# A decode layer on one core: feed-forward weights loaded last, gate and up in column form, another layout for w_down

## The chip, the cores and the metric

The kernel runs on one core of one Trainium2 chip. The metric is the device time of one execution in microseconds (us). A core has a tensor engine (PE, with its weight loads shown as PEld), a vector engine (DVE), a scalar engine (ACT), a general engine (POOL) and a sync engine (SP) that here issues the loads. Loads run on 16 DMA engines. "Span" is the time from the first to the last instruction in the profile; it is about 1.8 us shorter than the time. All runs quoted are in the fast state, and every kernel below gave a correct result.

## The reference, cut to what matters

One token, width 512. Attention over a cache of 65,536 positions with 32 query heads on 8 key/value heads of 128, then a gated feed-forward layer of 1,792 hidden units.

```python
x = A_x
h = x + attention(layernorm(x), k_cache, v_cache, wq, wo)   # K and V: 8 x 65536 x 128 bf16 each, 134 MB each
g = layernorm(h) @ w_gate        # 512 x 1792
u = layernorm(h) @ w_up          # 512 x 1792
out = h + (sigmoid(g) * u) @ w_down                          # 1792 x 512
```

Nearly all the bytes are K and V, each read once. The feed-forward weights are 3 x 1.83 = 5.5 MB of 282 MB.

## The kernel before

All loads go through one queue. K, V and w_q take turns in a ring of four slots of 4 MB; a load waits until the slot's last user is done. `Prog` writes operations down and derives the semaphore waits from the names in `deps`.

```python
order = [("wq", 0)]
order += [("K", b) for b in range(NR)]                 # NR = 4 blocks per head, NB = 32 blocks
for b in range(NR, NB):
    order += [("K", b), ("V", b - NR)]
order += [("V", NB - 4), ("wgu", 0), ("V", NB - 3), ("V", NB - 2), ("V", NB - 1)]
...
if k == "wq":
    ... # w_q into the ring, and directly behind it the whole of w_down into its own buffer:
    B_w_down[0:1536, :].rearrange("(c p r) n -> p c (r n)", p=128, r=4)   # wd0: 3 x 4 rows per partition
    B_w_down[1536:1792, :].rearrange("(p r) n -> p (r n)", r=2)           # wd1: 2 rows per partition
...
if ld == ("V", NB - 4):
    ... # w_o, in pieces of 1 KB, into the buffer that the scores no longer need
```

After the last V block: rest of PV, head output (`po`, `ox`, `o2`), projection with w_o, layer norm (`hc` is the centred row as a column), and the feed-forward layer in row form. There `hc` is the stationary operand of one column and the weights stream past, so the result is a row:

```python
for i, bank in enumerate((GB, UB)):                    # gate, up
    for kt in range(4):
        for c in range(4):                             # 512 columns each, on 4 strips of 32 PE columns
            matmul(ps(bank, 0, n, 32*c, 32*c+1), lhsT=hc[:, kt:kt+1], rhs=wv[:, kt, c*512:c*512+n], ...)
sg = tanh(rstd * gate)             # 128x512 on ACT       (the sigmoid by way of tanh)
up = rstd * up                     # 128x512 on DVE
hh = (sg + 1) * up                 # 128x512 on DVE
# 14 tiny matmuls turn the rows of hh into columns, 4 copies take them to hhT
for kt in range(14):
    for g in range(4):
        matmul(ps(YB, 0, 128, 32*g, 32*g+1), lhsT=hhT[:, kt:kt+1], rhs=wd_v[:, kt, g*128:(g+1)*128], ...)
# copy to y_sb, output DMA
```

## Time and profile before

| | before |
|---|---|
| time, median of 3 (then of 4) runs | 681.42 us (680.79) |
| span of the profiled run | 678.4 us |
| last V completion in the trace | 665.27 us |
| span behind it | 13.1 us |

Lines of the page of the kernel before: the span, the DMA share in 40 slices (9 is 90% or more), the rate in each slice, and the totals.

```profile
span 678.4 us, 5646 instructions
...
PE 391.9 (58%) x2506; PEld 158.8 (23%) x2506; DVE 353.6 (52%) x405; ACT 34.3 (5%) x92; POOL 5.7 (1%) x10
...
DMA  8999999999999999999999999999999999999990
GB/s 346 441 433 430 433 432 433 430 433 432 433 430 429 433 425 433 428 433 430 431 432 431 431 432 431 432 433 428 433 432 431 433 432 427 430 423 359 433 416 24
DMA packets 15640, 282.68 MB, mean 417 GB/s; under 512 B 1153, under 2 KB 5249, under 8 KB 6785
```

PE and DVE are busy little more than half of the time, and the stream of loads moves at about 432 GB/s from the second slice on. A kernel like this takes the time of the stream, plus what stands before the first byte, plus what stands behind the last. The last slice shows 24 GB/s: there nothing is loaded.

The windows view of the end of the stream. After the stretch and its length come busy time and count of PE, PEld, DVE, ACT and POOL, then the granted PE clock, the mean share of the 16 DMA engines and the rate.

```profile
659.00:660.00 1.00, 0.17 (x4) 0.00 (x0) 0.00 (x0) 0.00 (x0) 0.00 (x0) 0.65 0.97 410
...
661.00:662.00 1.00, 0.00 (x0) 0.00 (x0) 0.00 (x0) 0.00 (x0) 0.00 (x0) 1.00 0.54 229
...
663.00:664.00 1.00, 1.00 (x16) 0.36 (x16) 0.00 (x0) 0.00 (x0) 0.00 (x0) 0.56 0.12 49
...
665.00:666.00 1.00, 1.00 (x16) 0.15 (x8) 0.00 (x0) 0.00 (x0) 0.00 (x0) 0.50 0.00 0
```

The stream doesn't end at once. A load is split over 16 engines, and it has landed when the last of them is done. The 16 completions of the last V piece come in groups: seven at 661.1 to 661.6, seven at 663.0 to 663.5, two at 665.06 and 665.27.

The timeline of what follows (start, length, engine, line, operation, output and inputs, count):

```profile
662.87 3.50 PE L401 MATMUL PS<-ring,PT_sb 128*16 128x512 bf16 x32 [3.70 <-DMA ring<-in_A_v_cache_dram]
...
669.28 0.16 DVE L453 SCALAR_TENSOR_TENSOR hc<-PS,hT 128x4 bf16<-128x4 f32 x1 [0.48 <-PE PS L259]
...
669.50 2.76 PE L462 MATMUL PS<-ring,hc 128*1 128x512 bf16 x29 [0.25 <-DVE hc L453]
...
672.74 0.75 DVE L472 TENSOR_SCALAR up<-PS,rstd 128x512 f32<-128x512 f32 x1 [2.65 <-remote]
673.52 0.69 DVE L473 SCALAR_TENSOR_TENSOR hh<-sg,up 128x512 bf16<-128x512 f32 x1
...
674.27 0.32 PE L478 MATMUL PS<-ones_c,hh 1*128 1x1 bf16 x14 [1.16 <-DVE hh L473]
...
675.01 0.95 PE L491 MATMUL PS<-wd_sb,hhT 128*1 128x128 bf16 x56 [0.43 <-ACT hhT L487]
676.02 0.29 DVE L495 CAST y_sb<-PS 128x128 bf16<-128x128 f32 x1 [1.11 <-PE PS L491]
676.33 0.62 SPq L496 DMA_DIRECT2D out_dram<-y_sb  x1
```

Every step waits for the one before it, from V's landing to the output. All weights were in memory long before, so in these 13.1 us the DMA engines stand idle, but for the output.

### The profile page before, as it was taken

How to read it: one execution, taken by the hardware profiler on the slowest of the kernel's cores; microseconds unless marked ns; L12 is line 12 of the kernel's file. 1: busy time of each engine (PE TensorE's matmuls, PEld its weight loads, DVE VectorE, ACT ScalarE, POOL GpSimd, SP SyncE). 2: the span in 40 equal slices, each digit the busy share in tenths (PEclk: the TensorE clock that was granted, in tenths of full speed). 3: DMA queues.
4: the chain of work that ended last, by engine and by line, in shares of the span. 5: the costliest groups of instructions: out<-in, count | busy, mean ns of one | idle time of the engine just before them, and what ended most of it. 6: DMA issues, size and time to landing. Idle time of an engine off the chain costs nothing.

```text
span 678.4 us, 5646 instructions
## 1 busy us (share of the span) xinstructions
PE 391.9 (58%) x2506; PEld 158.8 (23%) x2506; DVE 353.6 (52%) x405; ACT 34.3 (5%) x92; POOL 5.7 (1%) x10
## 2 busy tenths in 40 slices
PE   2587596555566655455665655466665644662145
PEld 2432232122222222122222222122221212221112
DVE  3289875564447655463556744465555644470001
ACT  0200100020002000020000200020000200020000
POOL 3000000000000000000000000000000000000000
PEclk9889797777888767688887778887766778885567
DMA  8999999999999999999999999999999999999990
GB/s 346 441 433 430 433 432 433 430 433 432 433 430 429 433 425 433 428 433 430 431 432 431 431 432 431 432 433 428 433 432 431 433 432 427 430 423 359 433 416 24
DMA packets 15640, 282.68 MB, mean 417 GB/s; under 512 B 1153, under 2 KB 5249, under 8 KB 6785
## 3 DMA queue, kind: packets, MB, share of 16 engines
q1 hardware_dynamic: 15616, 282.34, 97.6%
q8 instruction: 19, 0.31, 0.2%
q14 instruction: 5, 0.03, 0.0%
HBM read 282.33 MB, written 0.00 MB: 416 GB/s over the span
## 4 chain that ended last, share of the span: by engine, by line
issue 98%; DVE 1%; PE 0%; another core or an unknown queue 0%; POOL 0%; POOLq 0%; ACT 0%; ACTq 0%; DVEq 0%
DVE rows_i L244 0%; PE PS L491 0%; DVE up L472 0%; DVE hh L473 0%; PE PS L259 0%; POOLq L112 0%; POOL rstd L270 0%; PE PS L478 0%; DVE lsel L247 0%; DVE y_sb L495 0%; DVE sel_f L248 0%; DVE zrow L239 0%; POOL iota_i L232 0%; DVE ident L236 0%
## 5 line engine op out<-in xcount | busy, mean ns | idle before, releaser
L338 PE MATMUL PS<-ktw 128*128 128x512 bf16 x1024 | 294.4, 449 | 205.7 <-DVE ktw L324 203.3
L324 DVE STREAM_TRANSPOSE ktw<-ring 128x1024 f32<-128x1024 f32 x256 | 292.0, 1208 | 192.7 <-DMA ring<-in_A_k_cache_dram 192.7
L338 PEld LDWEIGHTS PS<-ktw 128*128 128x128 bf16 x1024 | 107.0, 110 | 389.6 <-DVE ktw L324 249.9
L401 PE MATMUL PS<-ring,PT_sb 128*16 128x512 bf16 x1024 | 69.9, 420 | 28.0 <-DMA ring<-in_A_v_cache_dram 28.0
L325 DVE TENSOR_REDUCE M_sb<-PS 128x1 f32<-128x512 f32 x32 | 22.1, 692 | 47.5 <-PE PS L338 47.5
L401 PEld LDWEIGHTS PS<-ring,PT_sb 128*16 128x16 bf16 x1024 | 28.2, 113 | 60.1 <-DMA ring<-in_A_v_cache_dram 32.4
L415 DVE CAST O<-PS 128x4 bf16<-128x4 f32 x8 | 1.3, 163 | 57.5 <-PE PS L412 57.5
L358 ACT ACTIVATE negmax<-PS 128x1 f32<-128x1 f32 x8 | 1.4, 171 | 554.9 <-PE PS L356 554.9
L370 DVE STREAM_TRANSPOSE PT_sb<-P_sb 128x512 bf16<-128x512 bf16 x32 | 21.8, 712 | 11.9 <-ACT P_sb L367 11.9
L367 ACT ACTIVATE P_sb<-PS,negmax 128x512 bf16<-128x512 f32 x32 | 21.6, 686 | 0.3
L289 PE MATMUL PS<-ring,xz 128*32 128x128 bf16 x128 | 9.3, 248 | 6.4 <-DMA ring<-in_A_wq_dram 6.4
L289 PEld LDWEIGHTS PS<-ring,xz 128*32 128x32 bf16 x128 | 9.2, 113 | 6.5 <-issue 6.5
L425 PE MATMUL PS<-O,ktw 128*128 128x1 bf16 x128 | 3.7, 165 | 9.6 <-DMA ktw<-in_A_wo_dram 9.4
L412 PE MATMUL PS<-sel_bf,po_sb 128*128 128x4 bf16 x32 | 2.0, 167 | 12.4 <-ACT po_sb L409 12.4
L409 ACT ACTIVATE po_sb<-PS,rl 128x512 bf16<-128x512 f32 x8 | 5.6, 695 | 56.4 <-PE PS L401 56.4
L349 PE MATMUL PS<-identf,gm 128*1 128x128 f32 x16 | 3.0, 271 | 7.8 <-DVE gm L347 7.8
L270 POOL TENSOR_TENSOR rstd<-ve,nhalf 128x1 f32<-128x1 f32 x2 | 1.1, 553 | 664.4 <-DVE ve L268 664.4
L367 ACT ACTIVATION_READ_ACCUMULATOR P_sb<-PS,negmax 128x1 f32 x32 | 6.5, 203 | 0.0
L356 PE MATMUL PS<-one_f,gmrep 1*128 1x1 f32 x16 | 3.0, 256 | 5.0 <-DVE gmrep L353 5.0
L425 PEld LDWEIGHTS PS<-O,ktw 128*128 128x128 bf16 x128 | 3.5, 103 | 9.8 <-DMA ktw<-in_A_wo_dram 9.4
L412 PEld LDWEIGHTS PS<-sel_bf,po_sb 128*128 128x128 bf16 x32 | 1.3, 96 | 17.1 <-ACT po_sb L409 17.1
L351 DVE TENSOR_REDUCE gmj<-PS 1x4 f32<-1x128 f32 x8 | 2.2, 278 | 3.8 <-PE PS L349 3.8
(67 smaller groups left out, 50.3 us busy)
## 6 DMA issues: line engine op xcount, KB each, us to landing
ring<-in_A_k_cache_dram SPq DMA_DIRECT2D x32, 4096.0 KB, 29.7
ring<-in_A_v_cache_dram SPq DMA_DIRECT2D x31, 4096.0 KB, 35.4
ring<-in_A_wq_dram SPq DMA_DIRECT2D x1, 4096.0 KB, 12.4
ktw<-in_A_wo_dram SPq DMA_DIRECT2D x1, 4096.0 KB, 22.3
ring<-in_A_v_cache_dram SPq DMA_DIRECT2D x1, 3072.0 KB, 38.2
ring<-in_B_w_gate_dram SPq DMA_DIRECT2D x1, 1792.0 KB, 26.4
ring<-in_B_w_up_dram SPq DMA_DIRECT2D x1, 1792.0 KB, 14.8
wd_sb<-in_B_w_down_dram SPq DMA_DIRECT2D x1, 1536.0 KB, 15.8
```

What stands on the lines that cost most here:

```text
L289: op("pe", lambda e, kt=kt, n=n, last=last: e.matmul(ps(1, 0, 128, 0, 32), lhsT=xz[:, kt * 63 + 31 - n: kt * 63 + 63 - n], rhs=wq_v[:, kt, ...
L324: op("dve", lambda e, d=dst, sr=src: e.transpose(d, sr), deps, f"T{b}.{c}")
L325: op("dve", lambda e: e.tensor_reduce(M_sb[:, b % 8:b % 8 + 1], ps(b % NS, 0, 512), AX.X, ALU.max), [f"S{b}"], f"mx{b}")
L338: op("pe", lambda e, n=n, je=je, c=c: e.matmul(ps(b % NS, 0, 512), lhsT=w_ap(h, je, c), rhs=kt_ap(n, je), start=(c == 0 and je == 0), stop ...
L349: op("pe", lambda e: e.matmul(ps(MISC, 0, 128, 0, 1), lhsT=gm[:, k:k + 1], rhs=identf[:, :], start=True, stop=True), [f"gm{h}", "identf", ...
L356: op("pe", lambda e: e.matmul(ps(MISC, 128, 129), lhsT=gmrep[0:1, :], rhs=one_f[0:1, 0:1], start=True, stop=True), [f"gmrep{h}", "onef"], ...
L367: op("act", lambda e, b=b: e.activation(P_sb[:, (b % 4) * 512:(b % 4 + 1) * 512], ps(b % NS, 0, 512), AF.Exp, bias=negmax[:, k:k + 1], sca ...
L370: op("dve", lambda e, b=b: e.transpose(PT_sb[:, (b % 8) * 512:(b % 8 + 1) * 512], P_sb[:, (b % 4) * 512:(b % 4 + 1) * 512]), [f"E{b}", f"P ...
L401: op("pe", lambda e, lhsT=lhsT, tq=tq, t0=t0, c=c: e.matmul(ps(bank, 0, 512, 32 * tq, 32 * tq + 16), lhsT=lhsT, rhs=ring[:, s * SLOT + t0 ...
L409: op("act", lambda e: e.activation(po_sb[:, :], ps(PO_BANKS[k], 0, 512), AF.Copy, scale=rl[:, k:k + 1]), [f"PV{NR * h + NR - 1}", f"rl{h}" ...
L412: op("pe", lambda e, t=t: e.matmul(ps(MISC, 140, 144), lhsT=po_sb[:, t * 128:(t + 1) * 128], rhs=sel_bf[:, 4 * t:4 * t + 4], start=(t == 0 ...
L425: op("pe", lambda e, j=j, nt=nt, last=last: e.matmul(ps(YT, nt, nt + 1), lhsT=wo_v[:, j, nt * 128:(nt + 1) * 128], rhs=O2[:, j:j + 1], sta ...
```

## The change

The intent: let the feed-forward weights be the last loads, so that they stream in while the serial part after V runs; and give the feed-forward layer a form whose result is a column at once, so that neither turns nor wide activations stand behind the last load. The diff, cut to its core:

```diff
-        order += [("V", NB - 4), ("wgu", 0), ("V", NB - 3), ("V", NB - 2), ("V", NB - 1)]
+        order += [("V", NB - 4), ("V", NB - 3), ("V", NB - 2), ("V", NB - 1), ("wg", 0), ("wu", 0), ("wd", 0)]
...
-        dma("sp", lambda e: e.dma_start(x4[:, :], ...), "x", name="x")
+        dma("act", lambda e: e.dma_start(x4[:, :], ...), "x", name="x")
...   (w_down's two loads behind w_q are gone; each of gate and up gets its own slot and semaphore)
+            elif k == "wd":
+                src = B_w_down.rearrange("(p r) n -> p r n", p=128)          # 14 rows per partition
+                for i, (r0, r1) in enumerate([(0, 12), (12, 14)]):
+                    d2, sr = dst[:, r0*D:r1*D].rearrange("p (r n) -> p r n", n=D), src[:, r0:r1, :]
+                    if i == 1:
+                        d2, sr = dst[:, r0*D:r1*D], src.rearrange("(o p) r n -> o p (r n)", o=8)[:, :, r0*D:r1*D]
+                    dma("sp", lambda e, d2=d2, sr=sr: e.dma_start(d2, sr), f"wd{i}", ...)
...   (row form, turns and copies are gone)
+        for i, (nm, bank) in enumerate((("wg", GB), ("wu", UB))):
+            for r in range(14):
+                for kt in range(4):
+                    lhsT = bass.AP(tensor=ring, offset=s0 + kt*FF + r, ap=[[NSLOT*SLOT, 128], [14, 128]])
+                    matmul(ps(bank, r, r + 1), lhsT=lhsT, rhs=hc[:, kt:kt+1], start=(kt == 0), stop=(kt == 3))
+        sg  = tanh(rstd * gate)            # 128x14 on ACT
+        sg2 = (sg + 1) * rstd              # 128x14 on DVE
+        hhT = up * sg2                     # 128x14 on DVE, already in columns
```

Partition p holds the hidden units 14p to 14p+13. So the weights of one matmul are every 14th column of w_gate: steps of 14 elements, 28 bytes.

## The prediction

> **What bounds the kernel now.** The stream of loads. The page gives 282.68 MB at a mean 417 GB/s; nearly every slice from the second on shows about 432 GB/s, while PE is busy 58% and DVE 52%. The DMA queue's waits show SP waiting for DVE to free K slots (446 us in sum), but without a gap in the stream, so they cost nothing. Three places are slower: the first 3 us, the stretch of w_o (351 GB/s at 610 to 620 us), and the end. The windows view shows the DMA share falling to 0.71 at 660 us and 0.12 at 663: of the 16 completions of the last V piece, seven come at 661.1 to 661.6, seven at 663.0 to 663.5, two stragglers at 665.06 and 665.27. Then comes a serial tail, in the timeline: PV's rest to 666.4, head output, projection and layer norm (hc at 669.4), gate and up to 672.7, up and hh to 674.2, 14 turns and copies to 675.0, down to 676.0, copy, output DMA to 678.4. So 13.1 us of the 678.4 us span have no load under them.
>
> **What the change does.** No byte is removed; 5.5 MB of weights move behind V. At 432 GB/s this is 12.7 us, so V31 lands at about 652.1, and PV, head output, projection and norm (4.1 us to hc) run under the loading of the gate. Landings: hc ready 656.2, gate 656.3, up 660.6, 12 rows of w_down 664.2, the last 2 about 665.3. Attention starts about 4.2 us earlier without w_down before K0; that alone gains nothing.
>
> Gate and up become 2x56 matmuls with 128x128 weights. The projection has the same form at 28 ns each (112 in 3.06 us, windows view), so 1.6 us each: up done at 662.2. The activations shrink from 128x512 (0.69 to 0.75 us) to 128x14 (small DVE operations take 0.16 us); turns and copies vanish. hhT is ready near 662.7, before w_down. After the last landing remain 8 matmuls (0.3 us), copy 0.3, output 2.4: 3.1 instead of 13.1.
>
> x on ACT's queue lets w_q be issued at 0.74 instead of 1.18 us: 0.4 us.
>
> The last 2 rows are split by 8. The Trainium skill, "DMA: Bandwidth & Descriptors", section on why a DMA increments its semaphore by 16, says that the DMA then uses the lowest 8 engines. The two groups of completions fit that: the early ones get these 262 KB, about 1.2 us. If a straggler is among them, it ends 0.6 us later than with 16.
>
> **On the critical path.** 10 us of tail, plus 0.4, minus up to 0.6. Predicted span 668.5; time 671.4 us (1.5% less), range 669.4 to 674.0. Faster by over 2%: 0.04; within 2%: 0.95; slower: 0.01.
>
> **Right or wrong.** V31 lands near 652; gate starts near 656.3, up on its DMA; the final matmuls wait for w_down's DMA, not DVE; the stream has no gap; 3.1 us follow the last landing.
>
> **What would make it wrong.** The new weights are read with 28-byte steps. "SBUF — State Buffer", section on the DMA port swizzle, names 16-byte lines, each crossing of which costs; no trace here shows such a step for weights (8 bytes in the turns cost nothing: 14 in 0.23 us). At 60 ns each it is still hidden; at 110 ns the time would be 675.8. Also: stragglers lagging more in the new order, or w_down's issue, which waits for PV30, coming late (expected 651, needed about 660).

## The result

| | before | changed |
|---|---|---|
| time, median of 4 runs | 680.79 us (680.13 to 681.5) | 670.07 us (669.99 to 670.13) |
| ratio | | 0.9842, 95% interval 0.9825 to 0.9859 |
| span | 678.4 | 668.3 |
| last completion of a load | 665.27 | 664.72 |
| span behind it | 13.1 | 3.6 |

All outputs are right. The ratio is the mean time of one kernel's runs over that of the other's of the same rounds, so it isn't quite the ratio of the medians quoted. The change is clear of noise, and inside the 2% band that counts as "same". The medians differ by 10.7 us and the spans by 10.1, because the profiled run of the kernel before was one of its quicker ones (680.17 us); its runs spread over 1.4 us here, those of the changed kernel over 0.14. Times are compared by medians below, and spans only tell where the time goes.

The page of the changed kernel:

```profile
span 668.3 us, 5771 instructions
...
DMA  9999999999999999999999999999999999999996
GB/s 377 436 429 421 437 432 431 423 437 432 431 429 431 433 431 426 432 437 430 426 430 435 436 421 435 432 431 427 431 431 434 428 432 433 429 433 362 430 414 247
DMA packets 15384, 282.70 MB, mean 423 GB/s; under 512 B 1152, under 2 KB 5248, under 8 KB 6400
```

The bytes and the rate in the middle are the same. The last slice moved from 24 to 247 GB/s: the stream now reaches far into what was the idle end. Its timeline:

```profile
648.96 3.34 PE L400 MATMUL PS<-ring,PT_sb 128*16 128x512 bf16 x32 [3.73 <-DMA ring<-in_A_v_cache_dram]
...
655.23 0.16 DVE L451 SCALAR_TENSOR_TENSOR hc<-PS,hT 128x4 bf16<-128x4 f32 x1 [0.48 <-PE PS L258]
...
656.06 3.50 PE L460 MATMUL PS<-hc,ring 128*128 128x1 bf16 x56 [0.87 <-DVE ve L267]
...
660.47 3.52 PE L460 MATMUL PS<-hc,ring 128*128 128x1 bf16 x56 [0.38 <-DMA ring<-in_B_w_up_dram]
664.03 0.17 DVE L471 TENSOR_TENSOR hhT<-PS,sg 128x14 bf16<-128x14 f32 x1 [3.89 <-PE PS L460]
...
664.26 1.67 PE L476 MATMUL PS<-ring,hhT 128*1 128x128 bf16 x56 [0.26 <-DVE hhT L471]
665.97 0.29 DVE L480 CAST y_sb<-PS 128x128 bf16<-128x128 f32 x1 [1.77 <-PE PS L476]
666.29 0.66 SPq L481 DMA_DIRECT2D out_dram<-y_sb  x1
```

From the completions in the trace, V landed at 651.41, gate at 655.92, up at 660.42, the first 12 rows of w_down at 664.09 and the last two at 664.72. The gate matmuls carry the label of a layer-norm step (`ve`), but nothing of that feeds them; they start 0.14 us after gate's completion, so gate's DMA released them. The part from PV to `hc`, which cost 4 us in the open, now lies under the gate's load.

Two things in these lines aren't as predicted. The 56 matmuls of gate, and of up, take 3.5 us, not 1.6. And the down matmuls were released by DVE (hhT), 0.17 us after w_down had landed, not by the DMA. They also take 1.67 us, where before they took 0.95. The windows view of just these 56, before:

```profile
675.00:676.10 1.10, 0.95 (x56) 0.78 (x56) 0.08 (x1) 0.00 (x0) 0.00 (x0) 1.00 0.00 0
```

and in the changed kernel:

```profile
664.20:666.00 1.80, 1.67 (x56) 1.38 (x56) 0.03 (x2) 0.00 (x0) 0.00 (x0) 0.50 0.05 9
```

The granted PE clock was 1.00 in the first case and 0.50 in the second. The new layout of w_down isn't what costs: form_step8 below has the old layout and the old buffer, and down takes 1.66 us there, also at 0.50.

### The profile page after: what moved, and what is told of

Read it like the earlier page. It is cut to its first block, busy times and chain, and to the rows that moved or that the text cites. A ratio compares the mean times of both kernels' runs of the same rounds, so it can differ in the third digit from the quotient of the medians.

```text
span 668.3 us, 5771 instructions
## 1 busy us (share of the span) xinstructions
PE 397.0 (59%) x2572; PEld 165.3 (25%) x2572; DVE 352.2 (53%) x402; ACT 33.7 (5%) x90; POOL 5.7 (1%) x10
## 4 chain that ended last, share of the span: by engine, by line
DMA 69%; DVE 25%; PE 5%; issue 0%; ACT 0%; SPq 0%
DMA ring<-in_A_k_cache_dram 61%; DVE ktw L323 24%; DMA ring<-in_A_v_cache_dram 5%; DMA ring<-in_B_w_up_dram 4%; PE PS L337 3%; PE PS L460 1%; DVE M_sb L324 1%; PE PS L400 1%; DVE PT_sb L369 0%; PE PS L476 0%; ACT P_sb L366 0%; SPq L203 0%; PE PS L348 0%; PE PS L355 0%; SPq L228 0%
## 5 line engine op out<-in xcount | busy, mean ns | idle before, releaser
L460 PE MATMUL PS<-hc,ring 128*128 128x1 bf16 x112 | 7.0, 198 | 1.2 <-DVE ve L267 0.9
L460 PEld LDWEIGHTS PS<-hc,ring 128*128 128x128 bf16 x112 | 6.9, 159 | 1.8 <-DVE ve L267 0.9
```

Source lines behind the costliest of these rows:

```text
L460: op("pe", lambda e, lhsT=lhsT, kt=kt, r=r, bank=bank: e.matmul(ps(bank, r, r + 1), lhsT=lhsT, rhs=hc[:, kt:kt + 1], start=(kt == 0), stop ...
```

## The experiments

The theory: time = end of the stream + what stands behind its last landing. The order of the loads gives nearly all of the gain by hiding the serial part, and the column form matters only through the little that it leaves behind the last landing. The rival: the column form is faster in itself and the order merely allows it.

### Order alone

The old arithmetic; only the loads moved (w_down in its old layout, x still on SP).

```diff
+        order += [("V", NB - 4), ("V", NB - 3), ("V", NB - 2), ("V", NB - 1), ("wg", 0), ("wu", 0), ("wd", 0)]
-                       ["hc", "wgu0", "wgu1"] if kt == 0 and c == 0
+                       ["hc", "wg" if i == 0 else "wu"] if kt == 0 and c == 0
```

> The kernel before with only the loads moved: gate, up and w_down last, arithmetic in the old row form, x still on SP. Theory (the gain is that the serial part after V runs under the loads): V's last piece near 652, w_down's last near 665.2; gate matmuls from 656, up from 660.5; about 5 us of old form after it, span near 669.5 to 671, so 7.5 to 9 of the 10.1 us. Rival (the column form is what shortens the tail, the order only allows it): under 4 us of gain, span over 674.

Measured: 671.16 us (before 681.32 on the same chip), ratio 0.9852, span 669.2. That is 10.2 us; the changed form measured below (after_step8) came to 670.31. The timeline of its end:

```profile
656.28 1.87 PE L460 MATMUL PS<-ring,hc 128*1 128x512 bf16 x16 [0.38 <-DVE mo L263]
...
660.68 1.45 PE L460 MATMUL PS<-ring,hc 128*1 128x512 bf16 x13 [2.52 <-DMA ring<-in_B_w_up_dram]
...
665.13 1.66 PE L489 MATMUL PS<-ring,hhT 128*1 128x128 bf16 x56 [0.66 <-DMA ring<-in_B_w_down_dram]
...
667.16 0.62 SPq L494 DMA_DIRECT2D out_dram<-y_sb  x1
```

All that the old row form does after up's landing (660.63), with turns and wide activations, is over at 664.8, before w_down's last landing (664.99). The final matmuls wait for the DMA of w_down. So order alone brings over nine tenths of the change, and the rival falls. It gained slightly more than I had expected (span 669.5 to 671).

What the column form adds in the new order can be read from x_sp below, which has the same order and also issues x on SP: 670.38 us, so 0.8 us less than order_only. Even this is an upper bound, since order_only also starts its down matmuls only when both pieces of w_down are there, while the changed kernel starts at the first.

### Form alone

The old order of loads, with w_down still before K0, but as 14 rows per partition; gate and up in column form.

```diff
+                    lhsT = bass.AP(tensor=ring, offset=s0 + kt*FF + r, ap=[[NSLOT*SLOT, 128], [14, 128]])
+                    matmul(ps(bank, r, r + 1), lhsT=lhsT, rhs=hc[:, kt:kt+1], ...)      # loads as before
```

> The kernel before with only the arithmetic changed: loads in the old order, gate and up in column form with 28-byte steps, w_down as 14 rows per partition loaded before K0. Theory: exposed, the 112 weight loads cost 63 ns each, 7.0 us against 3.2 for the old gate and up, of which the dropped turns and shorter activations give back about 2.3 us, and down runs at the lower granted clock: span 679.5 to 681, slower than before by 1 to 2.5 us. Rival (the column form is faster in itself): span 677 or less.

Measured: 683.14 us against 681.32, ratio 1.0028 (1.0013 to 1.0043), span 681.4: slower by 1.8 us. That is the loss expected, with a span 0.4 us above the range given. Gate and up in its timeline:

```profile
669.54 3.52 PE L459 MATMUL PS<-hc,ring 128*128 128x1 bf16 x56 [0.26 <-DVE mo L263]
...
673.53 3.52 PE L459 MATMUL PS<-hc,ring 128*128 128x1 bf16 x56
```

In the open, the new form is slower than the old one: 7.0 us for gate and up, where the old form ran from 669.5 to 672.7.

### What the 63 ns per matmul are

3.52 us / 56 = 63 ns. The projection in the same column form with contiguous weights took 28 ns each, at the same granted clock of 0.50 (timeline of the kernel before):

```profile
626.93 3.15 PE L425 MATMUL PS<-O,ktw 128*128 128x1 bf16 x112 [9.37 <-DMA ktw<-in_A_wo_dram]
```

The Trainium skill, "SBUF — State Buffer", section "Door 1: The DMA port swizzle", says that SBUF is read in lines of 16 bytes and that each access that crosses to a new line pays. Steps of 28 bytes cross at every element. To test this, the hidden units were mapped as in the kernel before (four units per partition in three groups, then two), which gives steps of 8 and 4 bytes, and w_down's old loads.

```diff
-                    lhsT = bass.AP(tensor=ring, offset=s0 + kt*FF + r, ap=[[NSLOT*SLOT, 128], [14, 128]])
+                    q, stp = (r // 4 * 512 + r % 4, 4) if r < 12 else (1536 + r - 12, 2)
+                    lhsT = bass.AP(tensor=ring, offset=s0 + kt*FF + q, ap=[[NSLOT*SLOT, 128], [stp, 128]])
```

In the old order:

> As form_only, but hidden units mapped to partitions as before (4 and 2 rows of w_down per partition), so the weights are read in steps of 8 and 4 bytes instead of 28. If the step costs: weight loads near 28 to 32 ns each, gate and up 3.2 to 3.6 us together, span 3.4 us below form_only (676 to 677.5). If the 63 ns come from the column form or the clock and not from the step: the same as form_only within 0.5 us.

Measured: 680.29 us, span 678.6, 2.8 us below form_only. Gate and up:

```profile
669.82 1.98 PE L461 MATMUL PS<-hc,ring 128*128 128x1 bf16 x56 [0.26 <-DVE hc L452]
...
672.27 1.97 PE L461 MATMUL PS<-hc,ring 128*128 128x1 bf16 x56
```

That is 35 ns each instead of 63, at the same granted clock (0.50 in the windows of both). The starts of the matmuls in the traces show it more sharply, free of what the first and the last one add: they follow each other every 60 ns with steps of 28 bytes (changed kernel), every 33 ns with steps of 8 bytes, and every 27 ns with steps of 4 bytes, which are the last 8 of each 56 in form_step8; the projection with contiguous weights also has 27. So the step costs, as the skill says; the numbers are from here. That the line is 16 bytes long is not shown: no step between 8 and 28 was run. Against the kernel before, this form comes out about even: the ratio is 0.9985 (0.9969 to 1.0002). Dropping the turns is worth nothing clear while it stands in the open: by the timelines, from up's end to the start of down takes 0.3 us instead of 2.3, but gate and up take 4.4 us instead of 3.2, and down, at the lower clock, 1.66 instead of 0.95. The fall was somewhat smaller than the 3.4 us expected, because 35 ns isn't 28, and because V happened to land 0.3 us later (665.22 against 664.94).

The same mapping in the new order:

> The changed kernel with steps of 8 and 4 bytes instead of 28, and w_down loaded in pieces of 4 KB and 2 KB as before. If the step costs: up done near 662.2 instead of 664.0, hhT near 662.4; then the down matmuls wait for the DMA of w_down (664.1), not for DVE, and the span falls by only 0.1 to 0.3 us (668.0 to 668.2), because w_down's landing is the next limit. If the step doesn't cost: up still done at 664.0, span 668.3.

Measured: 670.31 us, span 668.3, as the changed kernel.

```profile
660.22 1.98 PE L459 MATMUL PS<-hc,ring 128*128 128x1 bf16 x56 [1.90 <-DMA ring<-in_B_w_up_dram]
...
664.03 1.85 PE L475 MATMUL PS<-ring,hhT 128*1 128x128 bf16 x56 [1.84 <-DMA ring<-in_B_w_down_dram]
```

Up is done 1.8 us earlier, and nothing is gained: the down matmuls now wait 1.84 us for w_down. In the changed kernel up's end and w_down's landing nearly coincide, so taking one away leaves the other. The span didn't fall by the 0.1 to 0.3 us expected.

### Smaller pieces of w_down

```diff
-    WD_SPLIT = [(0, 12), (12, 14)]
+    WD_SPLIT = [(0, 4), (4, 8), (8, 12), (12, 14)]        # on top of after_step8; one wait for each piece
```

> As after_step8, with the first 12 rows of w_down in three loads of 4 rows, each with its own wait. Theory (what is left is the wait of 56 matmuls for one landing of 12 rows, 1.85 us of PE after 664.0): 32 to 48 of the 56 matmuls run before the last landing (664.5), down ends near 664.9 instead of 665.9, span 667.2 to 667.5, 0.8 to 1.1 us below after_step8. Rival (the loads lose time by being smaller, or PE at the lower clock is the limit anyway): 668.2 or more.

Measured: 669.25 us, span 667.4.

```profile
660.26 1.97 PE L459 MATMUL PS<-hc,ring 128*128 128x1 bf16 x56 [1.93 <-DMA ring<-in_B_w_up_dram]
...
662.50 1.02 PE L475 MATMUL PS<-ring,hhT 128*1 128x128 bf16 x32 [0.26 <-DVE hhT L470]
...
664.00 1.01 PE L475 MATMUL PS<-ring,hhT 128*1 128x128 bf16 x24 [0.48 <-DMA ring<-in_B_w_down_dram]
```

32 of the 56 matmuls now run before the third piece lands (663.96); the last piece lands at 664.59 and down ends at 665.01 instead of 665.9. This version was run again beside the changed kernel on one chip.

> The changed kernel, unaltered, for comparison on one chip with the version of smaller steps and split w_down. Both readings of it so far say 670.0 to 670.3 us.

> The kernel of step8_split again, beside the changed kernel on the same chip. If the 0.8 us between them are real and not of the chip: 669.2 to 669.4, 0.7 to 1.0 us below the changed kernel, without overlap of their runs. If the chip made it: within 0.2 us.

Measured: 670.05 us (669.9 to 670.18) and 669.40 us (669.26 to 669.43), with before at 680.48. The runs don't overlap: 0.65 us, a little less than I had expected. It is the fastest version found, with smaller steps and smaller pieces together; neither the kernel before nor the changed one reaches it.

### w_down first, gate and up last

```diff
-        order += [..., ("V", NB - 1), ("wg", 0), ("wu", 0), ("wd", 0)]
+        order += [..., ("V", NB - 1), ("wg", 0), ("wu", 0)]      # w_down behind w_q, into its own buffer
```

> The changed kernel with w_down loaded before K0 as in the kernel before (own buffer, 14 rows per partition), gate and up still last. Theory (what counts is how much arithmetic stands behind the last landing): up's landing becomes the last, near 664.8; behind it up 3.5, hhT 0.2, down 1.7, copy and output 2.4: span 672.4 to 673, 4 to 4.7 us above the changed kernel. Rival (moving w_down away from the front is of no use, the earlier start of attention is lost anyway): 668.3 to 669.

Measured: 674.24 us, span 672.4. The stream ended at 664.44, as ever, but with up:

```profile
664.48 3.52 PE L456 MATMUL PS<-hc,ring 128*128 128x1 bf16 x56 [0.28 <-DMA ring<-in_B_w_up_dram]
...
668.27 1.66 PE L472 MATMUL PS<-wd_sb,hhT 128*1 128x128 bf16 x56 [0.27 <-DVE hhT L467]
```

So 4.2 us of the gain come from w_down, rather than up, being what lands last, with steps of 28 bytes; up's 3.5 us are most of it.

### x from ACT's queue

```diff
-        dma("act", lambda e: e.dma_start(x4[:, :], ...), "x", name="x")
+        dma("sp", lambda e: e.dma_start(x4[:, :], ...), "x", name="x")
```

> The changed kernel with x issued by SP again ahead of w_q. Theory: the whole stream starts 0.44 us later and nothing gives it back: w_q is issued at 1.18, the last landing near 665.2, span and time 0.3 to 0.5 us above the changed kernel. Rival: slack elsewhere absorbs it, no difference beyond 0.1 us.

Measured: 670.38 us, span 668.6, the last landing at 664.99: 0.3 us later than in the changed kernel, in the span, the landing and the median alike. w_q is issued at 1.18 again (0.74 in the changed kernel). The Trainium skill, "DMA: Bandwidth & Descriptors", section "Issuing engines are not separate DMA queues", says that issuing from a second engine "will only save the time on the sequencer it takes to initiate the DMA"; that is what is seen here.

### The split by 8

The prediction took the view of the last two rows split by 8 to confine that load to 8 engines. In the changed kernel's completions all 16 engines finish it 0.6 us behind the 12 rows (660.00 becomes 660.62, and so on to 664.09 and 664.72), so it wasn't confined.

```diff
-                    if i == 1:
-                        d2, sr = dst[:, r0*D:r1*D], src.rearrange("(o p) r n -> o p (r n)", o=8)[:, :, r0*D:r1*D]
```

> The changed kernel with the last 2 rows of w_down loaded by the plain form, as the first 12 are. If the view split by 8 is merged back into 128 rows on the way and does nothing: again 16 completions, 0.6 us behind those of the 12 rows, span within 0.2 us of 668.3. If it did confine the load to 8 engines: now a different pattern, 8 completions moving by 0.6 us or more.

Measured: 670.22 us, span 668.3, 16 completions from 660.62 to 664.65 behind 659.98 to 664.01. The same. The split by 8 does nothing.

A load that does run on 8 engines:

```diff
+                        for q in range(16):                    # 16 loads of 8 partitions
+                            dma("sp", ..., d2[8*q:8*q+8], sr[8*q:8*q+8], ...)
```

> The changed kernel with the last 2 rows of w_down as 16 loads of 8 partitions each, so that by the reading of the prediction only 8 of the 16 DMA engines carry them. In the changed kernel all 16 completions of this load came 0.6 us behind those of the load before, so the split by 8 did not confine it. If the 8 engines used are the early ones: the completions of these loads end before 664.1 (the last of the 12 rows), near 661.8. If they are the late ones: they end near 665.4. The span is 668.2 to 668.4 in the first case, since hhT is ready only at 664.2, and 668.5 to 669 in the second.

Measured: 672.37 us, span 670.7: slower, and outside both cases expected.

```profile
664.73 1.45 PE L480 MATMUL PS<-ring,hhT 128*1 128x128 bf16 x48 [0.73 <-DMA ring<-in_B_w_down_dram]
...
667.94 0.38 PE L480 MATMUL PS<-ring,hhT 128*1 128x128 bf16 x8 [1.76 <-DMA ring<-in_B_w_down_dram]
```

Each of the 16 loads left 9 records: one at issue (648.9 to 654.8) and eight later. This agrees with the Trainium skill, "DMA: Bandwidth & Descriptors", section "Why a DMA increments its semaphore by 16 and not by 1": the issuing engine posts the share of the engines that aren't used at once, and 8 engines were used. The last of the eight went on in steps of 0.2 us until 667.89, 16 times 0.2 us after the 12 rows had ended at 664.59. So one of the late engines is among these eight. The packets of 2 KB are recorded at 0.09 us each, and the last packet of all starts at 665.62, 2.3 us before the last completion (0.5 us in the changed kernel). It is the completions that come 0.2 us apart; what takes that time isn't shown.

### Why the 16 completions are spread

The completions of one load lie 4.1 us apart at the end (660.62 to 664.72), and only 0.6 us apart at the start (w_q, changed kernel). The 4.7 us in the expectation below run over both pieces of w_down (660.00 to 664.72). In the traces the spread grows by steps of about 1.4 us, one engine at a time, about where the profile has a packet of 16 KB on queue q8, a fetch of instructions. The engines are hardly idle after that (the DMA row of the page has 9 in every slice but the last), so an engine set back mostly stays behind. To test it, POOL, which is idle, got 3072 memsets that nothing waits for:

```diff
         ln_rstd(0, 0, 0, 1.0)
+        for i in range(3072):
+            op("pool", lambda e, i=i: e.memset(scratch[:, i:i + 1], 0.0))
```

> The changed kernel with 3072 one-element memsets on POOL, which is idle, early in the span; nothing waits for them. It tests what makes the completions of one load spread over 4.7 us at the end: the 16 KB fetches of instructions (20 in the changed kernel), each of which seems to set one DMA engine back by about 1.4 us for good. Theory: about 12 more fetches of 16 KB; more engines are set back, the last landing comes 0.5 to 2 us later than 664.7 and the span rises by the same. Rival (the spread has another cause): fetches rise, the last landing and the span stay within 0.2 us.

Measured: 681.39 us, span 679.3, 11 us slower than the changed kernel. The size of it is far outside what I expected. Of its page, the span and the queues of instructions:

```profile
span 679.3 us, 8843 instructions
...
q8 instruction: 20, 0.33, 0.2%
q14 instruction: 28, 0.23, 0.1%
```

q14 had 4 packets in the changed kernel: 24 more, of 8 KB each. POOL's timeline shows them as pauses after every 128 memsets:

```profile
15.41 4.27 POOL L283 MEMSET scratch<- 1x1 f32 x128 [0.77 <-issue]
20.92 4.27 POOL L283 MEMSET scratch<- 1x1 f32 x128 [1.24 <-issue]
```

In the completions, one single engine falls behind. Its distance to the middle of the 16 grows evenly from 0.3 us at 13 us to 16.2 us at 146 us (the memsets run from 8.6 to 139.6), and then grows no more; at 612 us it is still 13.2 us, since the others have lost time as well. At the last load it is 3.7 us: between 608 and 639 us the others fall back by about 10 us, where the page shows 315 and 279 GB/s instead of 432. So 24 fetches cost this one engine 16 us, 0.7 us each, though their packets are recorded at 0.31 us. That they all ran on it follows from its lag growing with them; the trace doesn't name engines. The last landing came at 675.70 instead of 664.72, and again 3.6 us of span follow it. The lag of the late engine is shown to come from the added instructions; that the 16 KB fetches on q8 do the same to other engines is inferred from where the steps are.

### All of them in one table

| kernel | last landing | span behind it | span | time, median |
|---|---|---|---|---|
| before | 665.27 (V) | 13.1 | 678.4 | 680.79 |
| form_only | 664.94 (V) | 16.5 | 681.4 | 683.14 |
| form_step8 | 665.22 (V) | 13.4 | 678.6 | 680.29 |
| wd_first | 664.44 (up) | 8.0 | 672.4 | 674.24 |
| order_only | 664.99 (w_down) | 4.2 | 669.2 | 671.16 |
| x_sp | 664.99 (w_down) | 3.6 | 668.6 | 670.38 |
| changed | 664.72 (w_down) | 3.6 | 668.3 | 670.07 |
| after_step8 | 664.53 (w_down) | 3.8 | 668.3 | 670.31 |
| step8_split | 664.59 (w_down) | 2.8 | 667.4 | 669.25 |
| wd1_8p | 667.89 (w_down) | 2.8 | 670.7 | 672.37 |
| more_instr | 675.70 (w_down) | 3.6 | 679.3 | 681.39 |

The second column is the span less the first. Apart from the last two, which disturb the DMA engines, the stream ends within 0.9 us whatever the order; nearly all of the difference is what stands behind it.

## Why the prediction was right, and where it wasn't

- **The time.** Predicted 671.4 us (669.4 to 674.0), measured 670.07; span 668.5 predicted, 668.3 measured. Right, and nearer in the span: the prediction took its 10 us off the median of the runs before, 681.42, but its span came from a quicker run of 680.17 us. Off that run it would have been 670.2.
- **What bounds the kernel, and that the order hides the serial part.** Right, and shown: order_only alone brings 10.2 us, form_only alone loses 1.8.
- **Landings.** V near 652.1 (measured 651.41), gate 656.3 (655.92), up 660.6 (660.42), w_down 664.2 and 665.3 (664.09 and 664.72). Right within 0.7 us.
- **That attention's earlier start gains nothing.** K0 landed at 22.92 instead of 29.09, and the stream still ended where it did; wd_first, which takes that start back, has the same end of stream (664.44).
- **"The projection has the same form at 28 ns each, so 1.6 us each: up done at 662.2."** This step failed. It costed a matmul by another of the same shape with contiguous weights. The step of 28 bytes makes it 63 ns, and up ended at 664.0. The prediction named this risk and put the harmless limit at 60 ns, which fits: at 63 ns up's end and w_down's landing met within 0.2 us.
- **"The final matmuls wait for w_down's DMA, not DVE."** Wrong by a hair, for the same reason: they waited for DVE, 0.17 us after the DMA.
- **"3.1 us follow the last landing."** Measured 3.6. The sum had 48 of the down matmuls done before the last landing, in the 1.1 us from 664.2 to 665.3; at the 17 ns each that they took before (0.95 us for 56) that was enough. But the two landings were only 0.6 us apart, and at the granted clock of 0.50 the matmuls took 30 ns each (1.67 us; 48 alone took 1.45 us in wd1_8p). The late hhT adds no more than the 0.17 us above: in after_step8 it is ready at 662.4, and 3.8 us remain. Step8_split, where 32 of the 56 run before, has 2.8.
- **"The last 2 rows are split by 8 [...] the DMA then uses the lowest 8 engines."** Wrong. All 16 were used, and the plain form gives the same. The penalty of up to 0.6 us that the prediction allowed for it didn't come, and this about cancelled the 0.5 us missing from the tail. So the sum was better than its terms, and that was luck.
- **x on ACT's queue.** 0.4 us predicted, 0.3 measured.

## What to carry to other kernels

In a kernel bound by its stream of loads, order the loads by how much serial work follows each landing: the load with the least behind it goes last, and the long dependent part goes under the loads of what it doesn't need yet. Cost the new form at the access pattern that it will have, not at that of a neighbour with the same shape, and where two waits end together, expect nothing from shortening one of them. Look at the 16 completions of a load as well as at its landing: the slowest engine is the one that counts, and even instructions on an idle engine can set it back.

## What the Trainium skill lacked or had wrong

- "Runtime: NRT & Kernel Launch", section "Instruction fetch mechanics", says that crossing to the next block of instructions costs one bump of a DMA tail, "mostly hidden", and speaks of blocks of 16 KiB. Here POOL's fetches were of 8 KB, one for each 128 memsets, and POOL paused for about 1.25 us at each. 24 of them set one DMA engine back by 16 us, 0.7 us each, and cost the kernel 11 us, since each load is divided over the engines and waits for the slowest. No page gives this cost to the loads.
- "SBUF — State Buffer", on its 16-byte lines, gives no cost for weight loads, and counts two accesses to a line as enough for full bandwidth. Here column-form matmuls with 128x128 weights followed each other every 27 ns with contiguous weights and with steps of 4 bytes, every 33 ns with steps of 8 bytes (two to a line, so not free) and every 60 ns with steps of 28 bytes, all at a granted clock of 0.50.
- "DMA: Bandwidth & Descriptors", on how many engines a DMA uses, says "as the instruction carries it", but not that a view whose two outer dimensions are contiguous may be merged before that: a source split as 8 x 16 rows still ran on 16 engines (16 completions, all 0.6 us later). A real load of 8 partitions ran on 8 (9 completions, one of them at issue).
